# Batch 0's last convolution chunks interleaved on four PSUM banks, two shorter lead-in products of zeros, one ReLU per group moved for the last groups

## The chip, the core and the metric

The kernel runs on one core of one Trainium2 chip. The metric is the device time of one execution in microseconds (us). The kernel before takes 323.69 us, the median of 3 runs (323.54, 323.69 and 323.79). One more execution was profiled; it took 323.61 us, and the recorded span of its instructions is 321.8 us.

Engine names are those of the profile: PE multiplies matrices, PEld is PE's weight load, DVE and ACT are the vector and the scalar engine, POOL is the general engine (here it issues the loads and makes some copies), SP issues the stores and the transposing DMAs.

## The reference

`x` is 8 batches of 4224 rows by 192 columns. Two stages follow each other; cut to what matters:

```python
# stage 1: a causal convolution over 7 rows, one softmaxed kernel for each of 8 heads of 24 columns
w = exp(weight - max) / (sum + 1e-9)                      # [8, 7]
y[b, s, head] = sum_k w[head, k] * x[b, s - 6 + k, head]  # zeros ahead of row 0

# stage 2: a mixer of rank 32 along the sequence, then a two-layer network along the columns
h = (y^T @ U) @ V            # per batch: 192 x 4224, U is 4224 x 32, V is 32 x 4224
u = y + h^T
out = u + max(u @ w_ch1, 0) @ w_ch2        # w_ch1: 192 x 768, w_ch2: 768 x 192
```

`U` is contracted over the whole sequence of a batch, so no row of `u` of a batch can be finished before the whole batch is convolved.

## The kernel before

**Tiles.** A batch is 33 tiles of 128 rows; all 8 batches are 264 tiles, worked in 33 groups of 8 tiles (`GT`, `NG`). In SBUF `x` lies in blocks of 64 rows: the first 32 blocks of a batch in partitions 0 to 63 (called `r = 0`), the other 34 in partitions 64 to 127 (`r = 1`). The convolution multiplies a 64 by 64 band matrix, made from the softmaxed weights, with a block (and a second one, `halo`, with the block before it). PE works as four 64 by 64 quarters here: `r` chooses the row half, `c` (even or odd block) the column half. Even and odd block go side by side, so matmuls come in pairs.

**Batch 0 starts the kernel, and comes in pieces.** `KP` names them: piece 0 is tiles 0 to 9 (`r = 0`) and 16 to 23 (`r = 1`); piece 1, the "second piece", is tiles 24 to 32 (`r = 1`, 9 tiles); piece 2, the "third", is tiles 10 to 15 (`r = 0`, 6 tiles). POOL issues the loads in the order: the two parts of piece 0, `U` (L123, L127), pieces 1 and 2, the four parts of `V` (L137), the two halves of `w_ch1` (`W1_sb`, L145), then the first part of batch 1, `w_ch2` and so on.

**The order around the change** is written out by hand, and each engine takes its instructions in that order:

1. `idle(4)`: four products of zeros on PE, 512 columns each (L163, L171). Then the two halves of the band matrices, `band_half(0)`, `idle(1, 2)`, `band_half(1)`: 7 products each over `pr` from DVE, copied to SBUF by ACT and DVE.
2. `conv0(...)` convolves piece 0 (L370). Stages 3 and 4 interleave a chunk of `r = 0` with one of `r = 1`.
3. `u_layout` (L262) brings `U` into its layout; it needs the loads of `U`.
4. `yT` (L567) transposes `y` tiles by a product with the identity into PSUM, for groups 0 and 1 of batch 0; `place` says which PSUM bank takes which (group, 64-column chunk, half). Six banks' worth are placed: `(0,0),(0,1)`; `(0,2),(1,2)`; `(1,0),(1,1)`, each for `n = 0` and `n = 1`.
5. `tt_mm` (L443) accumulates `y^T U` over the tiles of piece 0, then `conv` (L408) does the second and the third piece, then `tt_mm` does the tiles of piece 1.
6. `tt_split` (L457 on ACT, L458 on DVE) splits the sum into a high and a low bf16 part; `yT(1, 0)`; `tt_late` (L759) adds the tiles of piece 2; two products with `R4` (L832) add the split parts; `yT(1, 1, 2)`; `tt_done` (L463); `hT` (L585) adds `h^T` to the transposed `y`; `uT_out` copies the banks to `uT` by ACT and DVE (L254, L256).
7. From there the loop over `SLOTS` runs: `w1(g, pattern)` multiplies with `w_ch1` (L620) and applies the ReLU on ACT (L634) or DVE (L636), `w2` multiplies with `w_ch2` (L647) and adds `u` on DVE (L656). Other work (convolutions of later batches, `h`, transposes) stands between the `w2` blocks. The last slot is groups 30, 31 and 32: three `w1` in a row, then 24 tiles of `w2`, and nothing else.

**Banks.** `bank()` gives out 8 PSUM banks in turn; a bank is taken again when its last reader is done. In step 5, `work` is four banks that `u_layout` used first, `tp` a fifth. The four transposing banks of `place` before the convolution take the other three and the first of `work`, so the convolution has three: the second piece goes to `work[3], work[1], work[2], work[3]`, the third to `work[1], work[2], work[3]`.

**ReLU patterns.** `RELU` and `RELU0` (L605, L606) give for each of 6 pairs of 128x512 which engine does each half: "AD" one on ACT and one on DVE, "AA" both on ACT. `RELU` has 7 on ACT and 5 on DVE in each group, `RELU0` (group 1 alone) 9 and 3.

Of the kernel before, what the change touches and what calls it, by code (L numbers as in the profile page):

```python
# [9 lines left out]
BF16 = mybir.dt.bfloat16  # L10
# [4 lines left out]
def kernel(  # L15
# [10 lines left out]
    nc = tc.nc  # L26
    P = nc.NUM_PARTITIONS
    B, S, D = x.shape
    H, KC = weight.shape
    GS = D // H  # L30
    R = moe_U.shape[1]
    M4 = moe_w_ch1.shape[1]
    NT = S // P
# [4 lines left out]
    NG = NTT // GT  # L38
# [17 lines left out]
    def bank():  # L56
        return psp.tile([P, 512], F32, name="ps", tag="ps")
# [103 lines left out]
    def idle(n, w=4):  # L161
        for _ in range(n):
            nc.tensor.matmul(  # L163
                out=wps[:, 0 : w * P].rearrange("p (n t) -> p n t", t=P),
                lhsT=zz[:],
                rhs=zz[:].unsqueeze(1).to_broadcast([P, w, P]),
                start=True,
                stop=True,
            )

    idle(4)  # L171

# [77 lines left out]
    def evac(eng, out, in_):  # L252
        if eng == "A":
            nc.scalar.activation(out=out, in_=in_, func=ACT.Copy)  # L254
        else:
            nc.vector.tensor_copy(out=out, in_=in_)  # L256
# [98 lines left out]
                    pp[part][:, 0 : nk[part] * GS].rearrange("p (k a) -> p k a", a=GS),  # L355
                )

    def conv0(stages, ks):


        yt[0] = ys.tile([P, NT, D], BF16, name="y_sb")
        for stage in stages:
            pp = [bank() for _ in stage]
            for hh in range(2):
                for halo in range(2):
                    for (r, h0, _), p in zip(stage, pp):
                        h, nk = h0 + hh, ks[r][1]
                        for c in range(2):
                            st = 1 - halo + c
                            nc.tensor.matmul(  # L370
                                out=p[HB * c : HB * c + HB, 0 : nk * 2 * GS].rearrange(
                                    "p (k a) -> p k a", a=2 * GS
                                )[:, :, hh * GS : hh * GS + GS],
                                lhsT=bands[h // HQ][
                                    HB * r : HB * r + HB, h % HQ, HB * halo : HB * halo + HB
                                ],
                                rhs=xt[0][
                                    HB * r : HB * r + HB,
                                    st : st + 2 * nk - 1 : 2,
                                    h * GS : h * GS + GS,  # L380
                                ],
                                start=(halo == 0),
                                stop=(halo == 1),
                                tile_position=(HB * r, HB * c),
                            )
            for (r, h0, eng), p in zip(stage, pp):
                j0, nk = NB0 // 2 * r, ks[r][1]
                evac(
                    eng,
                    yt[0][:, j0 : j0 + nk, h0 * GS : h0 * GS + 2 * GS],  # L390
                    p[:, 0 : nk * 2 * GS].rearrange("p (k a) -> p k a", a=2 * GS),
                )

    def conv(b, h0, nh, rs, engs, ks=((0, NB0 // 2), (0, NB1 // 2)), pp=None):

        if yt[b] is None:
            yt[b] = ys.tile([P, NT, D], BF16, name="y_sb")
        nk = {r: ks[r][1] - ks[r][0] for r in rs}
        if pp is None:
            pp = {r: bank() for r in rs}  # L400
        w = nh * GS
        for hh in range(nh):
            h = h0 + hh
            for halo in range(2):
                for r in rs:
                    for c in range(2):
                        st = 1 - halo + c + 2 * ks[r][0]
                        last = nc.tensor.matmul(  # L408
                            out=pp[r][HB * c : HB * c + HB, 0 : nk[r] * w].rearrange(
                                "p (k a) -> p k a", a=w  # L410
                            )[:, :, hh * GS : hh * GS + GS],
                            lhsT=bands[h // HQ][
                                HB * r : HB * r + HB, h % HQ, HB * halo : HB * halo + HB
                            ],
                            rhs=xt[b][
                                HB * r : HB * r + HB,
                                st : st + 2 * nk[r] - 1 : 2,
                                h * GS : h * GS + GS,
                            ],
                            start=(halo == 0),  # L420
                            stop=(halo == 1),
                            tile_position=(HB * r, HB * c),
                        )
        for n, r in enumerate(rs):
            j0 = NB0 // 2 * r + ks[r][0]
            evac(
                engs[n % len(engs)],
                yt[b][:, j0 : j0 + nk[r], h0 * GS : h0 * GS + w],
                pp[r][:, 0 : nk[r] * w].rearrange("p (k a) -> p k a", a=w),
            )  # L430
        return last
# [21 lines left out]
    def tt_split(b, p):  # L453

        hi = sml.tile([P, D], BF16, name="tt_hi")
        lo = sml.tile([P, D], BF16, name="tt_lo")
        nc.scalar.activation(out=hi[:], in_=p[:, 0:D], func=ACT.Copy)  # L457
        nc.vector.tensor_tensor(out=lo[:], in0=p[:, 0:D], in1=hi[:], op=ALU.subtract)  # L458
        ttb[b] += [hi, lo]
# [92 lines left out]
    def place(p, n, *chunks):  # L552

        for k, (g, c) in enumerate(chunks):
            at0[g, c, n] = (p, 2 * P * k)
            for hf in range(2):
                last_of[id(p), hf] = (g, c, n)

    def yT(g, *cs):


        for c in cs:
            for n in range(2):
                p, o = at0[g, c, n]
                for i in range(2):
                    for hf in range(2):
                        nc.tensor.matmul(  # L567
                            out=p[HB * hf : HB * hf + HB, o + i * P : o + (i + 1) * P],
                            lhsT=yt[0][:, GT * g + 4 * hf + 2 * n + i, HB * c : HB * c + HB],
                            rhs=ident[:],  # L570
                            start=(id(p), hf) not in opened,
                            stop=False,
                            tile_position=(0, HB * hf),
                        )
                        opened.add((id(p), hf))
# [27 lines left out]
            )  # L603

    RELU = ["AD", "AD", "AA", "AD", "AD", "AD"]  # L605
    RELU0 = ["AA", "AD", "AA", "AD", "AA", "AD"]  # L606

    def w1(g, pat):
# [147 lines left out]
    def tt_late(p):  # L756

        for n, j in enumerate(late):
# [5 lines left out]
                stop=False,  # L764
            )

    conv0(
        [
            [(0, 0, "A")],
            [(0, 2, "A")],  # L770
            [(0, 4, "A"), (1, 0, "D")],
            [(0, 6, "A"), (1, 2, "D")],
            [(1, 4, "D")],
            [(1, 6, "A")],
        ],
        KP[0],
    )
    work = [bank() for _ in range(4)]
    tp = bank()
    u_layout(work)  # L780
# [30 lines left out]
    for n in range(2):  # L811
        place(bank(), n, (0, 0), (0, 1))
    yT(0, 0, 1)
    for n in range(2):
        place(bank(), n, (0, 2), (1, 2))
    yT(0, 2)
    early = piece_tiles(0) + piece_tiles(1)
    na = len(piece_tiles(0))
    tt_mm(0, early, tp, (0, na))
    for n, (h, k) in enumerate(zip(range(0, H, 2), (3, 1, 2, 3))):  # L820
        conv(0, h, 2, [1], "AD"[n % 2], KP[1], {1: work[k]})
    for n, (h, k) in enumerate(zip(range(0, H, 3), (1, 2, 3))):
        conv(0, h, min(3, H - h), [0], "AD"[n % 2], KP[2], {0: work[k]})
    tt_mm(0, early, tp, (na, len(early)))
    tt_split(0, tp)
    for n in range(2):
        place(bank(), n, (1, 0), (1, 1))
    yT(1, 0)
# [59 lines left out]

    for gs1, gs2, at in SLOTS:
        for g in gs1:  # L890
            ends = w1(g, RELU0 if g == 1 else RELU)
            for b, blocks in LOADS.items():
                for q, (gb, m) in enumerate(blocks):
                    if gb == g:
                        x_load(b, q, ends[m])
                        if steps:
                            steps.pop(0)()
            if g == 0:
                do("h2")
        while steps and gs1 != [3]:  # L900
            steps.pop(0)()
        npc = 4 * len(gs2)
        for p in range(npc + 1):
            for what in at.get(p, []):
                do(what)
            if p < npc:
                g, k = gs2[p // 4], p % 4
                if g == NG - 1 and k == 3:
                    w2(g, 6, 1)
                    w2(g, 7, 1)  # L910
                else:
                    w2(g, 2 * k, 2)
# [30 lines left out]
```

## Time and profile before

| quantity | value |
|---|---|
| runs, median (lowest to highest) | 323.69 us (323.54 to 323.79) |
| the profiled execution | 323.61 us |
| its span | 321.8 us (1.8 us lie around it) |
| PE, DVE, ACT, POOL busy | 98%, 83%, 53%, 44% |
| granted PE clock, mean over the span | 0.998 |
| lead-in up to the first product with `w_ch1` | 19.76 us |
| last `w1` stage (groups 30 to 32) | 294.31 to 306.14 us |
| last `w2` stage | 306.07 to 318.12 us |

A row of the page's part 5 reads: line, engine, operation, what it writes and reads, shape and count, then busy time and mean duration, then the time for which the engine stood idle just before, and who ended that. The chain that ended last is followed from the last instruction back to what released each step; "issue" in it is time in which the engine waited for nothing that the profile shows. A matmul's duration is some 0.2 us longer than its share of PE, because matmuls are pipelined; the distance from one start to the next is what one costs.

### The profile page before, as it was taken

The page shows a single profiled execution, that of the slowest core. Times are in us where ns is not written, and L with a number is a line of the kernel's source. Part 1 is how long each engine was busy: PE and PEld are TensorE (multiplying, and loading weights), DVE is VectorE, ACT ScalarE, POOL GpSimd, SP SyncE. Part 2 cuts the span into 40 slices and gives each one's busy share as a digit, 9 for nine tenths or more (in the row PEclk, how much of TensorE's full clock was granted, in tenths as well). Part 3 has the DMA queues.
Part 4 walks back from the last instruction along what each step waited for, and adds up shares of the span by engine and source line. Part 5 has one row for each costly group of instructions (what it writes and reads, how often), then busy time and mean ns, then how long its engine had stood idle before and what let it go on. Part 6 is the DMA issues. An engine that isn't in the chain of part 4 may idle for free.

```text
span 321.8 us, 9602 instructions
## 1 busy us (share of the span) xinstructions
PE 316.0 (98%) x4004; PEld 219.8 (68%) x4004; DVE 268.2 (83%) x551; ACT 169.5 (53%) x344; POOL 141.6 (44%) x108
## 2 busy tenths in 40 slices
PE   8999999999999999999999999999999999999995
PEld 4857576478677647946864884686596497497495
DVE  6779989987977986996998699699898888897863
ACT  2666723960874396088249509825804903903910
POOL 8663299529937982993798398000000000000000
PEclk9999999999999999999999999999999999999999
DMA  9999993997997999699699982178087078059035
GB/s 104 191 195 173 194 231 102 191 204 240 220 154 146 266 152 192 172 196 194 180 232 145 189 208 82 52 192 204 2 229 213 3 195 248 2 171 271 2 125 172
DMA packets 122443, 53.39 MB, mean 166 GB/s; under 512 B 87712, under 2 KB 122400, under 8 KB 122400
## 3 DMA queue, kind: packets, MB, share of 16 engines
q1 hardware_dynamic: 84528, 38.08, 46.0%
q0 software_dynamic: 37728, 14.60, 39.3%
q8 instruction: 31, 0.51, 0.7%
q14 instruction: 12, 0.10, 0.1%
q10 hardware_dynamic: 144, 0.10, 0.1%
HBM read 29.22 MB, written 25.95 MB: 171 GB/s over the span
## 4 chain that ended last, share of the span: by engine, by line
PE 91%; ACT 3%; DMA 2%; DVE 2%; POOL 1%; issue 1%; POOLq 0%
PE ps L647 42%; PE ps L620 39%; PE ps L342 3%; PE ps L500 3%; PE ps L443 2%; DMA Ur<-in_moe_U_dram 2%; ACT rl_sb L634 2%; ACT y_sb L254 1%; PE ps L408 1%; DVE u_sb L523 1%; POOL x_sb L79 1%; PE ps L567 1%; DVE rl_sb L636 1%; PE ps L469 0%; DVE out_sb L656 0%
## 5 line engine op out<-in xcount | busy, mean ns | idle before, releaser
L634 ACT ACTIVATE rl_sb<-ps 128x512 bf16<-128x512 f32 x233 | 124.3, 604 | 89.1 <-PE ps L620 77.6
L647 PE MATMUL ps<-W_sb,rl_sb 128*128 128x192 bf16 x1584 | 139.8, 246 | 0.2
L647 PEld LDWEIGHTS <-rl_sb 128*128 128x128 bf16 x1584 | 128.4, 98 | 12.2 <-issue 11.9
L620 PE MATMUL ps<-uT,W_sb 64*128 64x512 bf16 x1188 | 131.5, 376 | 0.3 <-DVE uT L256 0.2
L636 DVE TENSOR_SCALAR rl_sb<-ps 128x512 bf16<-128x512 f32 x163 | 105.7, 689 | 15.2 <-PE ps L620 14.9
L620 PEld LDWEIGHTS <-W_sb 64*128 64x128 bf16 x1188 | 61.2, 94 | 66.0 <-issue 3.0
L656 DVE TENSOR_TENSOR out_sb<-ps,u_sb 128x384 f32<-128x384 f32 (+1 forms) x133 | 69.5, 550 | 25.9 <-PE ps L647 25.0
L308 POOL COPY xb_sb<-x_sb 32x3072 bf16<-32x3072 bf16 (+1 forms) x24 | 67.7, 2822 | 1.1
L523 DVE TENSOR_TENSOR u_sb<-y_sb,ps 128x192 bf16<-128x192 bf16 (+1 forms) x168 | 65.8, 461 | 0.0
L296 POOL COPY xb_sb<-x_sb 128x3072 bf16<-128x3072 bf16 x12 | 32.9, 2744 | 41.1 <-PE ps L342 33.7
L254 ACT ACTIVATE y_sb<-ps 128x408 bf16<-128x408 f32 (+4 forms) x90 | 38.1, 517 | 12.2 <-PE ps L342 9.8
L79 POOL DMA_DIRECT2D x_sb<-in_x_dram x32 | 27.1, 853 | 13.1 <-PE ps L500 7.5
L256 DVE CAST y_sb<-ps 128x408 bf16<-128x408 f32 (+2 forms) x37 | 19.4, 569 | 1.6 <-PE ps L408 1.6
L457 ACT ACTIVATE tt_hi<-ps 128x192 bf16<-128x192 f32 x8 | 2.6, 331 | 26.9 <-PE ps L443 26.9
L500 PE MATMUL ps<-tt_sb,V_sb 32*128 32x192 bf16 x264 | 12.0, 245 | 0.0
L342 PE MATMUL ps<-xb_sb,band 64*32 64x384 bf16 x192 | 11.8, 332 | 0.0
L342 PE MATMUL ps<-x_sb,band 64*32 64x384 bf16 x192 | 11.8, 332 | 0.0
L500 PEld LDWEIGHTS <-V_sb 32*128 32x128 bf16 x264 | 5.8, 92 | 5.7 <-issue 5.5
L163 PE MATMUL ps<-zz 128*128 128x512 f32 (+1 forms) x10 | 6.9, 840 | 1.1 <-DVE zz L151 1.1
L443 PE MATMUL ps<-y_sb,U_sb 128*32 128x192 bf16 x258 | 7.6, 248 | 0.0
L342 PEld LDWEIGHTS <-band 64*32 64x32 bf16 x384 | 4.3, 89 | 4.7 <-issue 2.4
L443 PEld LDWEIGHTS <-U_sb 128*32 128x32 bf16 x258 | 5.4, 96 | 1.5 <-issue 0.8
(67 smaller groups left out, 69.7 us busy)
## 6 DMA issues: line engine op xcount, KB each, us to landing
out_dram<-out_sb SPq DMA_DIRECT2D x131, 192.0 KB, 2.9
x_sb<-in_x_dram POOLq DMA_DIRECT2D x14, 384.0 KB, 7.0
x_sb<-in_x_dram POOLq DMA_DIRECT2D x8, 432.0 KB, 7.3
x_sb<-in_x_dram POOLq DMA_DIRECT2D x8, 408.0 KB, 6.8
W_sb<-in_moe_w_ch_dram POOLq DMA_DIRECT2D x3, 288.0 KB, 7.8
uT<-u_sb SPq DMA_TRANSPOSE x31, 3.4
x_sb<-in_x_dram POOLq DMA_DIRECT2D x1, 480.0 KB, 5.8
x_sb<-in_x_dram POOLq DMA_DIRECT2D x1, 288.0 KB, 8.1
```

Of the source, the lines that this page charges most:

```text
L79: return nc.gpsimd.dma_start(out=xt[b][HB * r : HB * r + HB, s0:s1, :], in_=x[b, blk * HB : (blk + s1 - s0) * HB, :].rearrange("(j p) d -> ...
L254: nc.scalar.activation(out=out, in_=in_, func=ACT.Copy)
L296: nc.gpsimd.tensor_copy(out=xbt[b][:, s0:s1, :], in_=xt[b][:, s0 + 1 : s1 + 1, :])
L308: nc.gpsimd.tensor_copy(out=xbt[b][q, s0:s1, :], in_=xt[b][q, s0:s1, :])
L342: nc.tensor.matmul(out=pp[r][QB * cg : QB * cg + QB, 0 : nk[r] * GS], lhsT=w[hr], rhs=t[hr, st : st + 2 * nk[r] - 1 : 2, hs], start=True, ...
L500: last = nc.tensor.matmul(out=banks[pr][:, a * D : (a + 1) * D], lhsT=V_sb[32 * q : 32 * q + 32, (j // 8) * 2 + j % 2, :], rhs=ttb[b][32 * ...
L523: nc.vector.tensor_tensor(out=u_group(g)[:, i : i + n, :, hf, :], in0=yt[b][:, run[0] : run[0] + n, :].rearrange("p n (c k) -> p n c k", c=3),
L620: last = nc.tensor.matmul(out=pps[m][hf][:], lhsT=W1_sb[HB * hf : HB * hf + HB, c, m * P : (m + 1) * P], rhs=uTt[g][HB * hf : HB * hf + HB ...
L634: nc.scalar.activation(out=rl[:, m, hf, :], in_=pp[hf][:], func=ACT.Relu)
L636: nc.vector.tensor_scalar_max(out=rl[:, m, hf, :], in0=pp[hf][:], scalar1=0.0)
L647: last = nc.tensor.matmul(out=cps[:, a * D : (a + 1) * D], lhsT=rlt[g][:, m, hf, (i + a) * P : (i + a + 1) * P], rhs=W2_sb[:, m, :], start ...
L656: nc.vector.tensor_tensor(out=o[:, 0:n, :].rearrange("p n (c k) -> p n c k", c=3), in0=cps[:, 0 : n * D].rearrange("p (n c k) -> p n c k", ...
```

## The change

Five edits are in it.

- The fourth of the first products of zeros is 256 columns wide and not 512.
- `conv0` takes any parts with their own tile range, head count, engine and bank, and interleaves them product by product. Piece 0 is called as before, one call for each stage.
- The transposes `yT(0, 2)` of `n = 1` (four products) and the `place` of their bank move from ahead of the convolution of pieces 1 and 2 to behind `tt_split`. The convolution therefore has all four banks of `work`.
- Pieces 1 and 2 are convolved through `conv0`. The last chunk of piece 1 (heads 6 and 7, `r = 1`, ACT copies) and the first of piece 2 (heads 0 to 2, `r = 0`, DVE copies) are one call and take turns; the engines of the copies alternate the other way round (second piece DVE, ACT, DVE, ACT; third DVE, ACT, DVE).
- Groups 30, 31 and 32 use `RELU1`: 8 ReLUs on ACT and 4 on DVE.

```diff
-    idle(4)
+    idle(3)
+    idle(1, 2)
...
-    def conv0(stages, ks):
+    def conv0(*parts):
...
+        mms = []
+        for r, h0, nh, (k0, k1), eng, p in parts:
+            nk, w = k1 - k0, nh * GS
+            todo = []
+            for hh in range(nh):
                 for halo in range(2):
...
+                    todo.append((r, h0 + hh, hh, halo, k0, nk, w, p))
+            mms.append(todo)
+        for n in range(max(len(todo) for todo in mms)):
+            for todo in mms:
+                if n >= len(todo):
+                    continue
+                r, h, hh, halo, k0, nk, w, p = todo[n]
+                for c in range(2):
+                    st = 1 - halo + c + 2 * k0
+                    nc.tensor.matmul(
...
+        for r, h0, nh, (k0, k1), eng, p in parts:
+            j0, nk, w = NB0 // 2 * r + k0, k1 - k0, nh * GS
+            evac(
...
-    def yT(g, *cs):
+    def yT(g, *cs, ns=(0, 1)):
 
         for c in cs:
-            for n in range(2):
+            for n in ns:
...
     RELU = ["AD", "AD", "AA", "AD", "AD", "AD"]
+    RELU1 = ["AD", "AD", "AA", "AD", "AA", "AD"]
     RELU0 = ["AA", "AD", "AA", "AD", "AA", "AD"]
...
     yT(0, 0, 1)
-    for n in range(2):
-        place(bank(), n, (0, 2), (1, 2))
-    yT(0, 2)
+    place(bank(), 0, (0, 2), (1, 2))
+    yT(0, 2, ns=(0,))
     early = piece_tiles(0) + piece_tiles(1)
     na = len(piece_tiles(0))
     tt_mm(0, early, tp, (0, na))
-    for n, (h, k) in enumerate(zip(range(0, H, 2), (3, 1, 2, 3))):
-        conv(0, h, 2, [1], "AD"[n % 2], KP[1], {1: work[k]})
-    for n, (h, k) in enumerate(zip(range(0, H, 3), (1, 2, 3))):
-        conv(0, h, min(3, H - h), [0], "AD"[n % 2], KP[2], {0: work[k]})
+    kb, kc = KP[1][1], KP[2][0]
+    conv0((1, 0, 2, kb, "D", work[0]))
+    conv0((1, 2, 2, kb, "A", work[1]))
+    conv0((1, 4, 2, kb, "D", work[2]))
+    conv0((1, 6, 2, kb, "A", work[3]), (0, 0, 3, kc, "D", work[0]))
+    conv0((0, 3, 3, kc, "A", work[1]))
+    conv0((0, 6, 2, kc, "D", work[2]))
     tt_mm(0, early, tp, (na, len(early)))
     tt_split(0, tp)
+    place(bank(), 1, (0, 2), (1, 2))
+    yT(0, 2, ns=(1,))
     for n in range(2):
         place(bank(), n, (1, 0), (1, 1))
     yT(1, 0)
...
-            ends = w1(g, RELU0 if g == 1 else RELU)
+            ends = w1(g, RELU0 if g == 1 else RELU1 if g >= NG - 3 else RELU)
```

More of the change, by code (lines that the diff above doesn't have):

```diff
@@ L356, in conv32 @@
                 )
-    def conv0(stages, ks):
[L361 to L364, printed above, removed]
-                for halo in range(2):
[L366 to L392, printed above, removed]
@@ new lines, in conv0 @@
+    def conv0(*parts):
+        if yt[0] is None:
+            yt[0] = ys.tile([P, NT, D], BF16, name="y_sb")
+        mms = []
[3 more added lines that the diff above has]
+            for hh in range(nh):
+                for halo in range(2):
+                    todo.append((r, h0 + hh, hh, halo, k0, nk, w, p))
[8 more added lines that the diff above has]
+                    nc.tensor.matmul(
+                        out=p[HB * c : HB * c + HB, 0 : nk * w].rearrange(
+                            "p (k a) -> p k a", a=w
+                        )[:, :, hh * GS : hh * GS + GS],
+                        lhsT=bands[h // HQ][
+                            HB * r : HB * r + HB, h % HQ, HB * halo : HB * halo + HB
+                        ],
+                        rhs=xt[0][
+                            HB * r : HB * r + HB,
+                            st : st + 2 * nk - 1 : 2,
+                            h * GS : h * GS + GS,
+                        ],
+                        start=(halo == 0),
+                        stop=(halo == 1),
+                        tile_position=(HB * r, HB * c),
+                    )
+        for r, h0, nh, (k0, k1), eng, p in parts:
+            j0, nk, w = NB0 // 2 * r + k0, k1 - k0, nh * GS
+            evac(
+                eng,
+                yt[0][:, j0 : j0 + nk, h0 * GS : h0 * GS + w],
+                p[:, 0 : nk * w].rearrange("p (k a) -> p k a", a=w),
+            )
@@ L765, in tt_late @@
             )
[L767 to L777, printed above, removed]
+    for parts in (
+        ((0, 0, "A"),),
+        ((0, 2, "A"),),
+        ((0, 4, "A"), (1, 0, "D")),
+        ((0, 6, "A"), (1, 2, "D")),
+        ((1, 4, "D"),),
+        ((1, 6, "A"),),
+    ):
+        conv0(*[(r, h, 2, KP[0][r], eng, bank()) for r, h, eng in parts])
     work = [bank() for _ in range(4)]
```

## The prediction

> **What bounds the kernel now.** I read the page's shares first, then the chain of work that ended last, then the lead-in instruction by instruction.
>
> ```profile
> span 321.8 us, 9602 instructions
> PE 316.0 (98%) x4004; PEld 219.8 (68%) x4004; DVE 268.2 (83%) x551; ACT 169.5 (53%) x344; POOL 141.6 (44%) x108
> PE 91%; ACT 3%; DMA 2%; DVE 2%; POOL 1%; issue 1%; POOLq 0%
> ```
>
> PE is the bound, and from the first `w1` on (19.76 us) its only idle times above 0.02 us are four of 0.04 to 0.11 us, each released by ACT or DVE work that itself followed PE. So a lead-in shorter by t shortens the whole by t, and nothing else in reach of this change can do more. The chain through the lead-in:
>
> ```profile
> 5.12 5.80 DMA Ur<-in_moe_U_dram
> 10.93 0.14 issue
> 11.06 0.70 PE ps L262 x15
> ...
> 13.27 2.87 PE ps L408 x64
> 16.15 0.35 PE ps L443 x9
> 16.50 0.23 PE ps L567 x4
> 16.73 0.40 issue
> 17.14 0.30 PE ps L567 x4
> ...
> 19.19 0.44 DVE uT L256
> 19.63 0.14 issue
> 19.76 1.32 PE ps L620 x10
> ```
>
> Up to 11.06 the load of `U` sets the time, not PE. Then PE carries the chain, except for one hole of 0.40 us at 16.73 that nothing in the profile is named for. PE's own timeline and its weight loads show it as starts of 16.43 and 17.14 in the middle of `yT(1, 0)`:
>
> ```profile
> 16.08 0.42 PE L443 MATMUL ps<-y_sb,U_sb 128*32 128x192 bf16 x9
> 16.43 0.30 PE L567 MATMUL ps<-ident,y_sb 128*64 128x128 bf16 x4
> 17.14 0.30 PE L567 MATMUL ps<-ident,y_sb 128*64 128x128 bf16 x4 [0.40 <-issue]
> 17.13 0.14 PEld L567 LDWEIGHTS <-y_sb 128*64 128x64 bf16 x4 [0.57 <-issue]
> ```
>
> The matmul at 17.14 waits for a bank that DVE's last 128x432 copy (15.88 to 16.49) had freed 0.6 us before. What fits instead is the refill of PE's instructions. The DMA queue table has a queue of kind instruction:
>
> ```profile
> q8 instruction: 31, 0.51, 0.7%
> ```
>
> 31 packets, 0.51 MB, for some 8,000 PE instructions: 16 KB, or about 256 instructions, each. Placed in time, late packets start about every 256 instructions just as PE gets there, but the first, due near instruction 180 (11 us), starts at 14.76 and ends at 15.71, since until then the load queue keeps the DMA engines full. The hole stands at instruction 450 of the trace, some 270 after the first packet fell due. I read it as PE out of instructions until that packet was usable. It is not proved: 1.4 us lie between the packet's end and the restart.
>
> **The change part by part.** The sum is against the profiled execution's 323.61 us, 0.08 under the median 323.69.
>
> *Zeros.* Each 512-column product is two passes. Before 6.28 us a pass costs 0.85 us, after it 0.43 (PEld starts at 4.64, 5.50, 6.28, 6.71, 7.14), so the cut instruction falls in the fast part: it gives 0.43 us, and `band_half(0)` can start at 6.71, when its data is there too (DVE's `pr` ends 6.65). The covers are two loads. Stage 3 of the convolution needs the upper half of piece 0, issued at 2.28, landing 7.0 later at 9.28; before, it started at 9.39. So of 0.43 some 0.06 is left, and `u_layout` behind it waits for `U` until 10.93 anyway: gain 0. The extra ACT and DVE slack behind (copies of `y` and `U_sb`, on which the next products wait at 11.69, 12.48 and 12.76) is worth 0.05. Then piece 1 must have landed (13.08); 13.20 becomes 13.15.
>
> *Convolution.* Start to start a pair of 216 columns costs 0.0925 us, one of 144 costs 0.0625. Before: 16 of the first and 16 of the second are 2.48 us; with waits for banks (0.05 at 14.38, 0.06 at 14.83, 0.10 at 15.71) and starting costs it lasts from 13.20 to 16.08. After: 12 pairs to 14.26, the first pair of heads 6 and 7 to 14.35. The next pair in the turn is `r = 0` and needs the third piece, issued at 6.51, landing 8.1 later at 14.64, so PE waits 0.3 us with the rest of heads 6 and 7 queued behind it. From 14.69 the two chunks use different row halves; in stages 3 and 4 of piece 0, pairs of 240 and of 192 columns ran side by side at 0.103 and 0.083, each at its own pace. So 3 turns at 0.0925 and 2 pairs at 0.0625 end at 15.09, the last 10 pairs at 15.72. Banks no longer hold anything: `work[0]` is free at 14.4, `work[1]` at 14.7, `work[2]` at 15.1. The change of tile shape costs 0.15 (15.92 to 16.08 before): `tt_mm` starts at about 15.85 instead of 16.08, a gain of 0.23. ACT's copy of heads 6 and 7 (0.53 us from 15.2) is done by 15.75, just in time.
>
> *Moved transposes.* Four products leave a place where they were free (PE waits for `U_sb` at 12.48 and 12.76) and come to the path: 0.14 us at the 0.055 of a pair plus the first 0.08. Then `yT(1, 0)` for `n = 0` needs ACT's copy of heads 3 to 5 (ends 16.27), and for `n = 1` DVE's copy of heads 6 and 7 (288 columns, about 0.45 from 15.93). PE reaches that matmul at about 16.43; before it could have gone at 16.55. DVE's and ACT's queues behind (`tt_hi`, `tt_lo`) end near 17.2, where the product that reads `tt_lo` stands 0.8 us after this matmul.
>
> *The hole.* The moved products were ahead of this matmul before and still are: 436 PE instructions precede it in either program, so it is again the first one of the missing block. The packet's time is set by the loads, unchanged in order and size, and by when PE got near instruction 180, which is in stage 4 to `u_layout`: at most 0.06 earlier. The restart is then at 17.08 to 17.14: PE waits 0.65 instead of 0.40, and what was won is waited away. What follows is serial on PE and unchanged. Bounds: the hole ends at the same time (0), or moves with PE's work. In that case 2.63 us (17.14 to 19.76) after 16.43 would be 19.06, but the second half of `w_ch1` stops it:
>
> ```profile
> L145 POOL DMA_DIRECT2D W_sb<-in_moe_w_ch_dram x1: 627/627/627, 11.6 to 11.6; - x1
> DMA to landing us min/median/max: 7.8/7.8/7.8
> ```
>
> Issued at 11.64, it lands at 19.40, so the first product with `w_ch1` can't start before 19.44: the most that the lead-in can win is 0.32 us. I take 0.05, near the fixed end, as the row nearest to the packet is its own time.
>
> *ReLU.* Three ReLUs go from DVE to ACT where PE sets the pace:
>
> ```profile
> 294.31 11.83 PE L620 MATMUL ps<-uT,W_sb 64*128 64x512 bf16 x108
> 295.22 11.57 ACT L634 ACTIVATE rl_sb<-ps 128x512 bf16<-128x512 f32 x21 [12.99 <-PE ps L620]
> 25.01 4.51 ACT L634 ACTIVATE rl_sb<-ps 128x512 bf16<-128x512 f32 x9 [0.40 <-PE ps L620]
> ```
>
> PE gives a group of 36 in 3.92 us. ACT, pressed in group 1, starts one ReLU every 0.48 us (4.51 less the last one's 0.67, over 8), so 8 need 3.83. PE doesn't wait for it, before or after; DVE's next work, the first `out_sb` at 307.27, waits for PE. Gain 0, loss 0.
>
> Sum: 0 + 0.05 + 0 = 0.05 us; 323.56 on the profiled execution's footing, 323.64 on the median's. I say 323.6.
>
> [...]
>
> **The rivals.**
> *The hole goes with PE's work.* If the hole was something else (a wait that the profile has lost), PE runs through and gains until `w_ch1` lands: minus 0.32, so 323.29 to 323.37. For it: the 1.4 us between packet and restart. Against: no semaphore explains 0.6 us, and the place fits the count. [...]
> *ACT becomes the bound of the last `w1` stage.* It decides once ACT starts fewer than one ReLU per 0.490 us (3.92 over 8). If ReLUs could not overlap at all they would cost 0.604 each: 24 are 14.5 us against PE's 11.76; the four pairs of banks that PE can be ahead absorb 1.8 of the 2.7, and 1.0 us is left: 324.6. Against: 0.48 measured on nine in a row.
> *The refill comes later.* Each us of delay past 17.1 is a us of time, as PE has nothing else to do. The first packet came 3.6 us after its place in the program; the second, equally under loads, 3.9. That difference, 0.3, gives 323.9.
>
> **How the numbers follow.** A measurement of this kernel tells about 0.2%, 0.65 us, from no change. The forecast (hole ends where it did, 323.5 to 323.7) has 0.60; the hole gone, or half gone, 0.22; ACT the bound 0.03; refill later by about 0.3 us 0.05, by over 0.65 us 0.05; something that wins more than the landing of `w_ch1` allows 0.05. Faster by over 0.2% is the last alone, 0.05; slower is 0.08; the rest, 0.87, is within. The range goes from the full gain, 323.2 with the runs' own spread of 0.1, to the later refill, 324.0.
>
> **What would show it.** The products with `pr` start at 6.7, but `u_layout` still at 11.06. The first pair of heads 0 to 2 starts at 14.69, `tt_mm` near 15.85. A hole of about 0.65 us ends near 17.1, at the second half of `yT(1, 0)`, and L620 starts between 19.70 and 19.76. In the last stage ACT has 24 ReLUs, and PE still takes 11.8 us. I am wrong if that hole is absent and L620 starts at 19.44, if the first q8 packet moves by more than 0.1 us, or if PE idles between 294 and 306.

## The result and the profile after

The changed kernel took 324.23 us (median of 21 runs, 323.67 to 325.32), the kernel before 323.60 us beside it (21 runs, 323.36 to 324.28). The ratio is 1.0019, with a 95% interval of 1.0012 to 1.0026: slower by 0.63 us, and 0.23 us above the top of the predicted range. The profiled execution of the changed kernel took 324.16 us, that of before 323.61.

From the page of the kernel after: its span, PE's share, the two queues of kind instruction (packets, MB, share of 16 engines), and the shares of the chain that ended last.

```profile
span 322.4 us, 9601 instructions
PE 314.3 (97%) x4004; PEld 219.2 (68%) x4004; DVE 267.1 (83%) x549; ACT 169.9 (53%) x346; POOL 141.4 (44%) x108
...
q8 instruction: 31, 0.51, 0.7%
q14 instruction: 12, 0.10, 0.1%
...
PE 90%; ACT 3%; DMA 3%; DVE 2%; POOL 2%; issue 0%; POOLq 0%
```

PE is busy for 1.7 us less (the products of zeros ended earlier, see below) and the span is longer, so the loss is no PE work. The chain of the kernel after through the lead-in (start, length, what):

```profile
6.49 8.30 DMA x_sb<-in_x_dram
14.79 0.04 issue
14.83 1.19 PE ps L379 x36
16.02 0.37 PE ps L452 x9
16.39 0.02 issue
16.41 0.34 ACT tt_hi L466
16.75 0.02 issue
16.77 0.37 DVE tt_lo L467
17.14 0.14 issue
17.28 0.30 PE ps L576 x4
...
19.77 0.14 issue
19.90 1.32 PE ps L630 x10
```

The load of the third piece has taken the place of `U`'s load, since the chain now goes through the first pair of heads 0 to 2. The first product with `w_ch1` starts at 19.90 us; before it was 19.76. So 0.14 us of the 0.55 between the two spans are already there, and the same 0.14 to 0.15 is found at the last stages. PE's timeline of the kernel after, at the places that the prediction named:

```profile
7.11 0.62 PE L235 MATMUL ps<-pr,ident 128*128 128x152 bf16 x7 [1.38 <-DVE pr L224]
...
15.95 0.42 PE L452 MATMUL ps<-y_sb,U_sb 128*32 128x192 bf16 x9
16.30 0.41 PE L576 MATMUL ps<-ident,y_sb 128*64 128x128 bf16 x8
17.28 0.30 PE L576 MATMUL ps<-ident,y_sb 128*64 128x128 bf16 x4 [0.56 <-DVE tt_lo L467]
```

The hole is there, at the same place in the program, and longer: 0.56 us in place of 0.40. The profile names `tt_lo` for it, but `tt_lo` is read only by a product at 18.10; the copy that this matmul waits for had ended at 16.52. Nor does the restart follow `tt_lo` closely: over the eight profiles that name it, PE starts again 0.04 to 0.30 us after `tt_lo` has ended. And the last two stages of the kernel after:

```profile
294.46 11.83 PE L630 MATMUL ps<-uT,W_sb 64*128 64x512 bf16 x108
...
295.36 12.13 ACT L644 ACTIVATE rl_sb<-ps 128x512 bf16<-128x512 f32 x24 [12.99 <-PE ps L630]
...
306.22 12.05 PE L657 MATMUL ps<-W_sb,rl_sb 128*128 128x192 bf16 x144
...
317.32 1.35 DVE L666 TENSOR_TENSOR out_sb<-ps,u_sb 128x384 f32<-128x384 f32 x3 [0.43 <-PE ps L657]
318.70 0.37 ACTq L674 DMA_DIRECT2D out_dram<-out_sb  x1
```

24 ReLUs on ACT, and PE takes 11.83 us as before. The corresponding end of the kernel before:

```profile
317.18 1.35 DVE L656 TENSOR_TENSOR out_sb<-ps,u_sb 128x384 f32<-128x384 f32 x3 [0.43 <-PE ps L647]
318.56 0.37 ACTq L664 DMA_DIRECT2D out_dram<-out_sb  x1
```

The last add ends at 318.67 in the one and 318.52 in the other. From there to the end of the span it is 3.70 us after and 3.30 before: the other 0.40 us lie behind the last instruction of any computing engine, in the last stores. The DMA view from 319.8 to 321 us (40 slices of 0.03 us; GB/s, then the window's packets and queues), first of the kernel before:

```profile
GB/s 52 51 26 26 26 26 26 26 26 26 0 26 26 26 26 0 0 0 0 0 0 0 0 0 0 0 0 0 0 0 0 0 0 0 0 0 0 0 0 0
DMA packets 23, 0.01 MB, mean 10 GB/s; under 512 B 7, under 2 KB 23, under 8 KB 23
...
q10 hardware_dynamic: 16, 0.01, 2.2%
```

and of the kernel after:

```profile
GB/s 410 358 180 205 128 26 26 0 26 26 26 26 26 0 26 26 26 26 26 26 26 26 0 26 26 26 26 26 26 26 26 26 0 26 26 0 0 0 0 0
DMA packets 94, 0.06 MB, mean 49 GB/s; under 512 B 18, under 2 KB 94, under 8 KB 94
...
q10 hardware_dynamic: 71, 0.04, 11.1%
```

In both, the last part runs at a steady 26 GB/s in nearly every slice (22 on average from 319.90 before, and from 320.00 after), until 320.28 before and until 320.87 after. I read this as a single one of the 16 DMA engines, alone after the others have finished: from 318.9 to 319.6 us 360 GB/s were moved before and 357 after, and a sixteenth of that is 22. What else was on the engines while the last stores ran is one packet of q14, 8 KB of instructions (12 packets, 0.10 MB): 0.72 us from 318.35 to 319.07 before, 0.735 us from 319.00 to 319.73 after. Before, it began 0.17 us ahead of the last add's end; after, 0.33 us behind it, on top of the last stores. The trace does not tell which DMA engine a packet lies on, so that it is the one that then works alone is a reading; the runs below test where the packet falls and when the stores end, not the engine.

The theory that goes into the experiments: DVE has fewer instructions (711 before, 709 after, in the program: three ReLUs less, and one copy more since the convolution's copies alternate the other way round), so the point in its instructions at which the last block is fetched lies later against the last stores, and the packet holds up the share of them that goes through its DMA engine. The rivals: the lead-in edits cost the time; the ReLUs on ACT cost it by their place in the last groups. And for the hole in the lead-in: it is PE's own instruction refill (the prediction's reading), or it hangs on the matmul at which it stands.

### The profile page after: what moved, and what is told of

Read it like the earlier page. It is cut to its first block, busy times and chain, and to the rows that moved or that the text cites. A ratio compares the mean times of both kernels' runs of the same rounds, so it can differ in the third digit from the quotient of the medians.

```text
span 322.4 us, 9601 instructions
## 1 busy us (share of the span) xinstructions
PE 314.3 (97%) x4004; PEld 219.2 (68%) x4004; DVE 267.1 (83%) x549; ACT 169.9 (53%) x346; POOL 141.4 (44%) x108
## 4 chain that ended last, share of the span: by engine, by line
PE 90%; ACT 3%; DMA 3%; DVE 2%; POOL 2%; issue 0%; POOLq 0%
PE ps L657 42%; PE ps L630 39%; PE ps L343 3%; PE ps L509 3%; DMA x_sb<-in_x_dram 3%; PE ps L452 2%; ACT rl_sb L644 2%; ACT y_sb L255 1%; POOL x_sb L79 1%; DVE u_sb L532 1%; DVE rl_sb L646 1%; PE ps L379 0%; PE ps L478 0%; PE ps L576 0%; DVE out_sb L666 0%
## 5 line engine op out<-in xcount | busy, mean ns | idle before, releaser
L646 DVE TENSOR_SCALAR rl_sb<-ps 128x512 bf16<-128x512 f32 x160 | 103.8, 689 | 17.1 <-PE ps L630 16.7
L297 POOL COPY xb_sb<-x_sb 128x3072 bf16<-128x3072 bf16 x12 | 32.9, 2742 | 40.8 <-PE ps L343 33.8
L255 ACT ACTIVATE y_sb<-ps 128x384 bf16<-128x384 f32 (+3 forms) x89 | 37.6, 520 | 12.4 <-PE ps L343 9.8
L257 DVE CAST y_sb<-ps 128x408 bf16<-128x408 f32 (+3 forms) x38 | 19.9, 566 | 1.2 <-PE ps L379 0.9
L163 PE MATMUL ps<-zz 128*128 128x512 f32 (+1 forms) x10 | 5.3, 674 | 1.1 <-DVE zz L151 1.1
```

The lines of the kernel that those rows point to most:

```text
L297: nc.gpsimd.tensor_copy(out=xbt[b][:, s0:s1, :], in_=xt[b][:, s0 + 1 : s1 + 1, :])
L646: nc.vector.tensor_scalar_max(out=rl[:, m, hf, :], in0=pp[hf][:], scalar1=0.0)
```

## The experiments

All kernels compute the whole output. Each ran beside the kernel before, whose median was 323.63 to 323.67 us. "Packet" is the start of the last q14 packet ahead of the span's end, "store" the end of the last store issued by ACT, both in us from the end of DVE's last add in the profiled execution. The column "704th" says what DVE's 704th record in the trace is (the trace has two fewer than the program). In every profile but the three with 708 instructions the packet starts 0.1 to 0.9 us after that record's end; in those three it starts 0.5 to 0.8 us before it.

| kernel | DVE instructions | 704th | packet | store | median us | ratio (95%) |
|---|---|---|---|---|---|---|
| `e2_after_old_relu` | 712 | last add but one | -0.18 | 1.58 | 323.57 | 0.9990 (0.9976 to 1.0003) |
| before | 711 | semaphore behind that add | -0.17 | 1.76 | 323.60 | |
| `e3b_after_plus2` | 711 | the same | -0.03 | 1.70 | 323.72 | 0.9994 (0.9980 to 1.0008) |
| after | 709 | drain behind the last add | +0.33 | 2.20 | 324.23 | 1.0019 (1.0012 to 1.0026) |
| `f3_relu_two_middle` | 709 | the same | +0.37 | 2.30 | 324.27 | 1.0017 (1.0009 to 1.0026) |
| `e1_relu_only` | 708 | closing semaphore | +1.43 | 1.36 | 323.22 | 0.9981 (0.9969 to 0.9993) |
| `e5_relu_middle` | 708 | the same | +1.76 | 1.35 | 323.18 | 0.9991 (0.9975 to 1.0006) |
| `f1_after_one_less` | 708 | the same | +1.68 | 1.35 | 323.11 | 0.9984 (0.9975 to 0.9993) |

The other six kernels below have 711 or more DVE instructions. Their packets begin 0.20 us ahead of that add's end to 0.11 behind it (with 723: 6.13 ahead), and their last stores end 1.49 to 1.81 us after it.

### The ReLU edit and the rest, apart

The kernel before with the ReLU edit alone:

```diff
+    RELU1 = ["AD", "AD", "AA", "AD", "AA", "AD"]
...
-            ends = w1(g, RELU0 if g == 1 else RELU)
+            ends = w1(g, RELU0 if g == 1 else RELU1 if g >= NG - 3 else RELU)
```

> The kernel before with RELU1 for groups 30 to 32 and nothing else of the change. Theory: DVE issues 3 instructions fewer (708 against 711), so its last refill of instructions (the 8 KB packet of q14 at 318.35 before) comes 0.5 to 1 us later, in front of the last stores on one DMA engine, and the landing of the last store moves from 2.2 us after its issue to 2.6 to 2.9. Time: +0.4 to +0.7 us (ratio 1.0012 to 1.0022); last DVE add and PE unchanged. Rival 1 (the ReLUs cost ACT or PE time): PE's w1 stage gets longer than 11.83 us. Rival 2 (the lead-in lost the time): no change, ratio 1.0000.

It was not slower but 0.45 us faster. The expectation had the direction wrong, and the profile fits the count: with 708 instructions the packet came 1.43 us after the last add, when all stores were done (they ended 1.36 us after it). The third instruction fewer carried the packet past the stores altogether: the 704th is now the semaphore instruction behind the drain, whose record stands at 320.64, after the stores and also after the packet (319.86).

The kernel after without the ReLU edit:

```diff
-            ends = w1(g, RELU0 if g == 1 else RELU1 if g >= NG - 3 else RELU)
+            ends = w1(g, RELU0 if g == 1 else RELU)
```

> The changed kernel with RELU in place of RELU1 for groups 30 to 32. DVE has 712 instructions, one more than before. Theory: the last q14 packet starts 0.2 to 0.5 us earlier than before's, relative to the last DVE add, and the last store lands in 2.2 us or less; time -0.3 to +0.1 us against before (ratio 0.9990 to 1.0003), and the first product with w_ch1 at 19.7 to 19.9 us. Rival 2 (the lead-in lost the time): ratio 1.0019, as for the whole change.

323.57 us, no difference from before that can be told (the interval goes from 0.8 us faster to 0.1 slower). The lead-in edits and the zeros together don't cost the 0.63 us, so the rival that blames the lead-in falls; whether they win something is not told. The two halves of the change, each at or below zero, together make +0.63: that is no sum of costs, and it fits a position. What the two halves change together is the count: 711 + 1 - 3 = 709.

### The count alone

To move the count without touching a ReLU, two and then fourteen small memsets on DVE were put into the last three groups of the kernel after, written into a tile of their own:

```diff
+    scr = cst.tile([P, 16], F32, name="scr")
...
+            for k in range(PADS[(g - NG + 3) * MC + m] if g >= NG - 3 else 0):
+                nc.vector.memset(scr[0:32, k : k + 1], 0.0)
```

> The changed kernel, all five edits, plus two one-column memsets on DVE in the last w1 stage, where DVE is idle, so that DVE has 711 instructions as before. Theory: the last q14 packet is back at 0.2 us ahead of the last DVE add and the last store lands in 2.2 us; ratio 0.9997 to 1.0005 against before, though two instructions were only added. Rivals 1 and 2: ratio 1.0019, as the whole change is still there.

> The changed kernel plus fourteen such memsets (723 DVE instructions, 12 more than before). Theory: the last q14 packet comes some 6 us before the end, where a store has slack, and no packet stands in front of the last stores: the last store lands in under 2.0 us, and the time is 0.3 to 0.5 us below before (ratio 0.9984 to 0.9992). Rivals 1 and 2: 1.0019 or a little more.

Both runs failed as a test of the time. The first took 326.79 us (1.0093, 1.0058 to 1.0128), the second 324.83 (1.0032, 1.0014 to 1.0050), with a new wait of 2.41 and 2.03 us in their profiles at 48.9 and 48.5 us, far from any memset. The second's tail still speaks: with 14 instructions more the packet came at 314.04, 6.13 us before the last add, and the last store ended 1.49 us after it. That is just below the 1.52 to 1.81 of packets close to that add's end, and above the 1.35 of those behind the stores, so a packet just ahead of the stores can cost little, and what makes up the last 0.14 us is open. The 704th is a semaphore instruction at 313.89 there. Against the two memsets of the next run that is 6.1 us for 12 instructions, 0.5 us each, and DVE has one `out_sb` add and one semaphore instruction in every 0.99 us. The packet follows DVE's instructions one for one; ACT's were untouched, so the block is DVE's.

The same two memsets without the tile, into `rq`, which nothing reads any more:

```diff
+            for _ in range(PADS[(g - NG + 3) * MC + m] if g >= NG - 3 else 0):
+                nc.vector.memset(rq[0:QB, 0:1], 0.0)
```

> The changed kernel with all five edits plus two one-column DVE memsets in the last w1 stage, written to the finished tile rq so that no tile is added (711 DVE instructions, as before). Theory (DVE's last refill stands in front of the last stores): its q14 packet goes back to 0.2 us ahead of the last DVE add, the last store ends 1.6 to 1.8 us after that add and not 2.2, and the time is that of before, ratio 0.9990 to 1.0005. Rival (the lead-in or the ReLUs on ACT cost it): ratio 1.0015 to 1.0022, as for the whole change.

323.72 us: two idle instructions more on DVE take 0.5 us off the kernel after. Packet and last store are back where they were before (-0.03 and 1.70).

### The count, with the ReLUs elsewhere

The kernel before with the ReLU edit in three groups in the middle, and with it in two:

```diff
+    RELU1 = ["AD", "AD", "AA", "AD", "AA", "AD"]
...
-            ends = w1(g, RELU0 if g == 1 else RELU)
+            ends = w1(g, RELU0 if g == 1 else RELU1 if 12 <= g <= 14 else RELU)
```

```diff
+    RELU1 = ["AD", "AD", "AA", "AD", "AA", "AD"]
...
-            ends = w1(g, RELU0 if g == 1 else RELU)
+            ends = w1(g, RELU0 if g == 1 else RELU1 if 13 <= g <= 14 else RELU)
```

> The kernel before with the RELU1 pattern in groups 12 to 14 and the old one in groups 30 to 32 (708 DVE instructions; the last stages are as before). Theory (only the count of DVE instructions ahead of the end matters): q14's last packet of the run falls behind the last stores, as it did with the pattern in groups 30 to 32 (319.86, 1.4 us after the last DVE add); the last store ends 1.3 to 1.5 us after that add, ratio 0.9975 to 0.9992. Rival (the three ReLUs help by leaving DVE free at the end): no change, 0.9996 to 1.0004.

> The kernel before with the RELU1 pattern in groups 13 and 14 alone: 709 DVE instructions, the count of the changed kernel, and nothing of its lead-in or its last stage. Theory: DVE's last refill starts 0.3 to 0.5 us after the last DVE add, the last store ends 2.1 to 2.3 us after it, and the time is that of the changed kernel, 324.0 to 324.3 (ratio 1.0010 to 1.0020), though one ReLU more in the same place (708) gave 323.18. Rival (fewer DVE instructions are simply better): 323.3.

Three moved ReLUs, 708: 323.18 us, with the same tail as with the edit in the last groups (store at 1.35 and 1.36). Its interval includes 1, so its time alone does not decide; the tail does. Two, 709: 324.27 us, slower by 0.64 us, as the kernel after, with none of its other edits, and its ReLUs moved around 145 us. So the place of the ReLUs does not explain the loss and the count does; the rival that blames ACT in the last groups falls.

### One instruction fewer

The kernel after with the ReLU edit in the last four groups:

```diff
-            ends = w1(g, RELU0 if g == 1 else RELU1 if g >= NG - 3 else RELU)
+            ends = w1(g, RELU0 if g == 1 else RELU1 if g >= NG - 4 else RELU)
```

> The changed kernel with the RELU1 pattern in the last four groups and not three: one ReLU more on ACT, one DVE instruction fewer (708). Theory: like the kernel before with RELU1 alone (also 708), DVE's last refill falls behind the last stores; the last store ends 1.3 to 1.5 us after the last DVE add and not 2.2, and the time is 323.1 to 323.4 us, 0.8 to 1.1 below the changed kernel and 0.3 to 0.5 below before. Rival (the change's lead-in costs 0.1 to 0.2 us that the other two effects hide): 323.4 to 323.6.

323.11 us (322.93 to 323.45), the fastest of all: 0.52 us below the kernel before, and 1.1 us below the kernel after, by one ReLU. Its DMA view from 319.8 to 321 us:

```profile
GB/s 0 0 0 0 0 0 0 0 273 0 0 0 0 0 0 0 0 0 0 0 0 0 0 0 0 0 0 0 0 0 0 0 0 0 0 0 0 0 0 0
DMA packets 1, 0.01 MB, mean 7 GB/s; under 512 B 0, under 2 KB 0, under 8 KB 0
...
q14 instruction: 1, 0.01, 1.6%
```

No store is left in the window; the one packet is DVE's block, and it runs alone. Beside `e1_relu_only` with the same count, 323.22, the lead-in edits are worth 0.1 us by the medians; the two intervals, each 0.3 to 0.4 us to either side, don't tell that from nothing.

### The lead-in

The zeros alone, on the kernel before:

```diff
-    idle(4)
+    idle(3)
+    idle(1, 2)
```

> The kernel before with the narrower fourth product of zeros alone. Expected by the recorded prediction: the first products start up to 0.4 us earlier unless DVE's data is late, the layout of U still waits for its load, the time is the same within 0.2 us (ratio 0.9995 to 1.0005); DVE's count (711) and its last refill's place are as before. Rival (PE's rate rises later): ratio 1.001 or more and the clock's step later than 6.6 us.

323.61 us, 0.9996 (0.9987 to 1.0005): nothing that can be told, as forecast. Its profile shows the forecast path too: the products with `pr` start at 6.70, and stage 3 of the convolution then waits for its load until 9.51.

For the hole, twenty more PE instructions ahead of it (ten products of 128 columns, each with its load of weights, for the fourth product of zeros; 19 more in the program, 16 more in the trace, where that product stands as two matmuls and two loads). If the hole hangs on the matmul at which it stands, it stays there; if it hangs on the count of PE's instructions, it moves to an earlier place in the program:

```diff
+    zb = zz[:].bitcast(BF16)
+
+    def idle_small(n, w=P):
+        for _ in range(n):
+            nc.tensor.matmul(
+                out=wps[:, 0:w], lhsT=zb[:, 0:P], rhs=zb[:, 0:w], start=True, stop=True
+            )
...
-    idle(4)
+    idle(3)
+    idle_small(10)
```

> The kernel before with the fourth 512-column product of zeros replaced by ten bf16 products of 128 columns, each with its own weight load: 19 PE instructions more ahead of everything. [...] Time unchanged within 0.3 us. Rival (the hole is a lost wait of yT(1, 0)): it stays at the second half of yT(1, 0).

PE's timeline of this kernel around the hole:

```profile
16.63 0.34 PE L451 MATMUL ps<-y_sb,U_sb 128*32 128x192 bf16 x5
17.77 0.27 PE L451 MATMUL ps<-y_sb,U_sb 128*32 128x192 bf16 x4 [0.81 <-issue]
17.97 0.41 PE L575 MATMUL ps<-ident,y_sb 128*64 128x128 bf16 x8
```

The hole has left the transposes and now splits the nine products of `tt_mm`. In the program it moved ahead by 16 recorded instructions, as many as were added; in the trace it is again at PE's 450th. So it hangs on the count. The other profiles show that its end hangs on the packet: in thirteen of the fourteen, PE starts its 450th 1.38 to 1.59 us after the end of q8's first packet, however early it got there (the fourteenth is the next kernel). In `e1_relu_only`, where PE got there last against the packet, it went on after 0.21 us (16.71 to 16.92) and the row shows no idle time. Count and packet together I read as PE's refill. How many instructions PE holds is not shown by any run; what they show is the 450th record. The time, 324.82 us (1.0037, 1.0017 to 1.0058), is 1.2 us above the kernel before, more than was expected: in this kernel the loads of `x` and `U` for batch 0 landed about 0.6 us later (the first part of `x` at 7.68, before at 7.07), for a reason that stays open, and its runs spread from 323.82 to 326.61.

Fifty such products in place of all four (96 PE instructions more), to have the refill asked for earlier:

```diff
...
-    idle(4)
+    idle_small(50)
```

> The kernel before with all four 512-column products of zeros replaced by fifty bf16 products of 128 columns with their weight loads: 96 PE instructions more ahead of everything. [...] Rival (no refill): the hole stays in yT(1, 0), no change.

325.02 us (1.0041, 1.0015 to 1.0067): 1.4 us slower than before, where a gain was looked for. The packet came earlier, at 13.01 in place of 14.76, and the hole at the 450th is gone as such. But the third piece of `x` landed at 15.53, 0.9 us later than before; the packet lasts 0.9 us. PE's timeline and a table of three stretches (length, each engine's busy time and count, the granted clock, the DMA share, GB/s):

```profile
12.99 1.73 PE L415 MATMUL ps<-x_sb,band 64*64 64x216 bf16 x32
15.57 1.56 PE L415 MATMUL ps<-x_sb,band 64*64 64x144 bf16 x32 [0.84 <-DMA x_sb<-in_x_dram]
17.06 0.66 PE L450 MATMUL ps<-y_sb,U_sb 128*32 128x192 bf16 x9
```

```profile
12.00:16.20 4.20, 3.33 (x84) 2.80 (x80) 1.98 (x6) 1.38 (x5) 2.40 (x5) 1.00 1.47 196
16.20:19.70 3.50, 3.50 (x47) 2.47 (x45) 0.97 (x2) 1.25 (x3) 3.50 (x6) 0.51 1.33 201
19.70:24.00 4.30, 4.09 (x66) 2.27 (x68) 3.56 (x8) 3.15 (x9) 2.30 (x10) 1.00 1.61 189
```

PE waits 0.84 us for that piece, and then its granted clock is 0.51 on average from 16.20 to 19.70 (it is down from 16.23 to 19.64); the first product with `w_ch1` starts at 21.23. I read it so that what the refill gains the load loses, and that more is lost with the clock. Both are inferred from this one profile, the first from the two times of 0.9 us, the second from the order of wait and clock (in `e7_zeros_plus20` PE waited 0.81 us at 17.77, and its clock stayed at 1.00 up to 24.00); four of this kernel's twelve runs are at 323.6 to 323.7 and others go up to 328.1.

### The tile that made the new wait

To tell the tile from the memsets of the two failed runs, the kernel before with the tile (64 bytes in each partition) and one early memset:

```diff
+    scr = cst.tile([P, 16], F32, name="scr")
+    nc.vector.memset(scr[0:32, 0:1], 0.0)
```

> The kernel before with one more SBUF tile of 64 bytes per partition ahead of the later tiles of its pool, and one early memset into it; nothing else. If the 2.0 to 2.4 us that PE waited at 48.5 us in the two kernels with such a tile came from the moved addresses, the second transposing DMA lands 8 us after its issue and not 4.3, and the time is 1 to 3 us over before. If it came from the memsets in the last stage, no wait there and 323.3 to 323.7.

325.48 us (1.0053, 1.0039 to 1.0067). Its timeline at the new wait, and its transposing DMAs from 38 to 52 us (count, median us from issue to landing):

```profile
40.80 2.51 SPq L546 DMA_TRANSPOSE uT<-u_sb  x1
...
46.54 0.42 PE L502 MATMUL ps<-tt_sb,V_sb 32*128 32x192 bf16 x8
49.12 3.20 PE L622 MATMUL ps<-uT,W_sb 64*128 64x512 bf16 x28 [2.16 <-DMA uT<-u_sb]
```

```profile
uT<-u_sb SPq DMA_TRANSPOSE x2, 6.7
```

The same rows of the kernel before:

```profile
40.38 1.40 SPq L544 DMA_TRANSPOSE uT<-u_sb  x1
...
46.11 0.42 PE L500 MATMUL ps<-tt_sb,V_sb 32*128 32x192 bf16 x8
46.46 4.41 PE L620 MATMUL ps<-uT,W_sb 64*128 64x512 bf16 x36
```

```profile
uT<-u_sb SPq DMA_TRANSPOSE x2, 3.7
```

The tile and its one memset are enough to make the wait. By the program the tile stands ahead of the later tiles of its pool and should move them by 64 bytes; the trace has no addresses. What it has is the DMA: the transposing one issued at 40.8 takes 2.51 us to issue in place of 1.40, and lands 8.3 us after its issue in place of 4.3. In the three profiles with the tile it lands 8.1 to 8.5 us after its issue, in the eleven without it 4.1 to 6.6. It can be late without the tile as well: in `f2_zeros_alone`, with 6.6 us, PE waits 0.45 us for it. Whether it is an address, and which tile's, was not tried.

## Why the prediction was wrong

**The step that failed is "ReLU", "Gain 0, loss 0".** Its working held: 24 ReLUs on ACT in 12.13 us, no PE wait between 294 and 306 us, PE at 11.83 us. But it priced what the edit does to the engines, and not what it does to DVE's instruction stream. The sum ended with PE's last product; what lies behind it, the stores, had no term, although 3.7 us of the profiled span lay there (318.12 to 321.82), 3.3 of them behind the last add. The "Convolution" part left out the same thing: its copies alternate the other way round, and that is one DVE instruction more. Two instructions fewer are worth +0.6 us (709), three -0.5 (708). How the packet holds up the stores, by sharing one DMA engine with them, is a reading that no run shows directly; that the count moves the packet, the last store's end and the time together is shown. The prediction had the mechanism in hand for PE, as the hole, and read q8's row; the row below it, q14, was not read.

**Zeros: gain 0** was right as a time (323.61 alone). In the changed kernel's profile its path was another: the products with `pr` started at 7.11 in place of 6.7, as `w_sb` landed at 4.52 in that execution (3.64 before) and `pr` came late. The passes of zeros were over sooner than forecast, since the fast ones (0.43 us a pass, 0.85 ahead of them) began with the first record of full granted clock, at 3.89 there and at 6.20 before, so PE had been idle for 1.38 us. `u_layout` started 0.13 us after `U` had landed (11.16 after 11.03), as before (11.06 after 10.93): the load covers all of this. In `f2_zeros_alone` the start was the forecast one.

**Convolution: gain 0.23.** The first pair of heads 0 to 2 began at 14.83 (14.69 forecast), set by the third piece as forecast, which landed at 14.79 and not 14.64; `tt_mm` at 15.95 (15.85), 0.13 us earlier than before and not 0.23. From that landing on it took 1.16 us, and 1.21 had been worked out: the step held, the load was later.

**The hole** ended 17.28 (17.08 to 17.14 forecast), after 0.56 us of waiting (0.65). That it hangs on PE's count and on q8's first packet is now shown by `e7_zeros_plus20` (16 recorded instructions more, and it stands 16 earlier in the program) and by the thirteen profiles (it ends 1.38 to 1.59 us after the packet); that this is the refill is the reading that fits both. The packet began from 14.40 to 14.88, or up to 15.29 with the two kernels whose loads were late (`e7_zeros_plus20`, `f4_tile_alone`). The 0.14 us by which this execution is later lies inside that spread. The gain of 0.05 in the lead-in is neither shown nor excluded.

PE's packets are 16 KB each (0.51 MB in 31). The later ones did not hold PE up in the kernel after: behind the first product with `w_ch1` PE is never idle for more than 0.11 us there. The first one goes with a wait of up to 0.8 us at PE's 450th recorded instruction (0.81 in `e7_zeros_plus20`). The packets on q14 are 8 KB each (0.10 MB in 12), and one of them at the wrong place goes with 0.6 us more time, without any computing engine waiting for it.

**The floor at 19.44** was wrong as well. The second half of `w_ch1` does not hold the first product: in `e1_relu_only` it started at 19.55 with that half landing at 19.68, in `e5_relu_middle` at 19.66 with 19.80.

**The rivals.** The hole did not go with PE's work; ACT was not the bound; the refill was not later by more than its spread. None of them was what happened. The range was built from them and had no term for the stores, so it did not hold the result.

## What to carry to other kernels

Where an edit changes how many instructions an engine has, look at the queues of kind instruction and at where their last packets fall against the last stores: a kernel whose end waits for stores can win or lose by one instruction (1.1 us here between `after` and `f1_after_one_less`), and a test with idle instructions tells this from the cost of the work. A span has a part behind the last instruction of the bounding engine; a sum that ends with that engine leaves it out (3.7 us here, from PE's end at 318.12 to the span's). And a test that adds a tile can cost more than what is tested (1.85 us here for the tile alone, against 0.63 for the whole change): write idle work into a finished tile.

## What the runs showed of the hardware that was not expected

- DVE's last block of instructions ahead of the end is one packet of 8 KB that takes 0.3 to 0.8 us. It starts 0.1 to 0.9 us after DVE's 704th instruction in the trace has ended, in eleven of fourteen profiles. Where it falls on the last stores, they end 2.20 to 2.30 us after the last add; 1.52 to 1.81 where it begins within 0.2 us of the add's end; 1.35 where it comes behind them. In the three kernels with 708 it began 0.08, 0.34 and 0.40 us after the last store had ended, which fits a 704th that waits for the stores; its record is only later (320.55 to 320.75), so this link is inferred.
- PE starts its 450th instruction of the trace, whatever that instruction is, 1.38 to 1.59 us after the end of a 16 KB packet (thirteen of fourteen profiles), and runs dry until then, for up to 0.8 us, when it gets there sooner. In the fourteenth, where the packet was asked for earlier, the load that PE needs next landed 0.9 us later.
- With 64 bytes more in each partition a transposing DMA landed 8.1 to 8.5 us after its issue (three kernels), without them 4.1 to 6.6 (eleven), and the kernels with them took 1 to 3 us longer.
- After a wait of 0.84 us in the lead-in PE's granted clock was down to 0.51 for 3.4 us (one execution of `e8_zeros_plus100`); after one of 0.81 us in `e7_zeros_plus20` it was not (1.00 from 16.20 to 24.00).
